# The first batch's prologue by halves of the heads, and the output products of two batches term by term

## The chip, the cores and the metric

The kernel runs on one core of one Trainium2 chip. The metric is the device time of one execution in microseconds (us); lower is better. A core has five engines that run side by side and wait for each other through semaphores: TensorE (PE in the profile; PEld is its loading of weights), VectorE (DVE), ScalarE (ACT), GpSimd (POOL, which does almost nothing here) and SyncE (SP, which here only issues loads and stores). Sixteen DMA engines move data between the chip's main memory and the on-chip memory; loads are issued from SyncE's queue (SPq) or ScalarE's (ACTq). TensorE writes its products into PSUM, which VectorE and ScalarE read.

## The reference

Attention against 32 learned memory slots for each head, followed by a gated feed-forward layer. There are 8 batches, 8 heads, 576 positions and 64 values for each head.

```python
a = phi - np.max(phi, axis=2, keepdims=True)          # (8, 8, 576, 32), over the positions
a = np.exp(a)
a = a / (np.sum(a, axis=2, keepdims=True) + 1e-09)
k_m = np.einsum('bhsm,bhsd->bhmd', a, k)
v_m = np.einsum('bhsm,bhsd->bhmd', a, v)
scores = scale * np.matmul(q, k_m.transpose(0, 1, 3, 2))
scores = scores - np.max(scores, axis=-1, keepdims=True)
attn = np.exp(scores)
attn = attn / (np.sum(attn, axis=-1, keepdims=True) + 1e-09)
attn_out = np.matmul(attn, v_m)
x = attn_out.transpose(0, 2, 1, 3).reshape(B * S, H * D)     # (4608, 512)
h = x @ w_in                                           # (4608, 2048)
g = h * (1.0 / (1.0 + np.exp(-h)))
out = g @ w_out                                        # (4608, 512)
```

w_in (512 x 2048) and w_out (2048 x 512) come as 64-bit floating-point numbers, everything else as 32-bit.

## The kernel before

**Precision.** The large products run in a shortened 32-bit format (fp32r). Each operand is split into a high part and the low rest, and three products stand for one: high by high, high by low, low by high. In the code these are the terms 0, 1 and 2 of `ffn2`: term 0 is g high by w_out high, term 1 g high by w_out low (`wo_lo`), term 2 g low by w_out high. The small products of the attention are plain fp32; in the trace each of them stands as two instructions, a transpose as one.

**Weights.** The two weight matrices are loaded as pairs of 32-bit words in blocks (`w_load`; "i0" is the first block of w_in, "o0" of w_out, each with two parts) and put together on chip by `w_conv`, whose steps are letters: p and c on ScalarE, s (a shift) and a (an addition) on VectorE, and for w_out h (the high part, ScalarE) and l (the low part, VectorE). `I0`, `O0` and `I1` are the first blocks.

**Order of work.** The eight batches are worked through one after the other. For a batch, the attention weights times w_in need only the product of the memory values with w_in (`p_mm`, its splitting `p_split`), and then the hidden product `ffn1` (tile `h`, line 701), the activation (`silu`), its splitting (`split`), and the output products (`main_step`, `ffn2`, line 746) into four PSUM tiles `acc` of 128 positions each. This runs in 16 steps `fc` of 128 hidden values. The output products of one step are issued behind the hidden product of the next (`finish`): in batch 0 in two pairs of tiles, in batch 1 all four tiles together. The other batches use another form of the output product (`st_step`, line 893). The attention of batch b + 1 is worked out in the shadow of batch b.

**The prologue.** For the first batch nothing can hide the attention; it is a prologue, written out by hand. Inside it TensorE, VectorE and ScalarE each keep the order of the program text (`in_order`). The heads are in two groups p (or g) of four: even and odd heads; k, v and q hold the groups side by side: group g of q and of the transposed memory keys lies on partitions 64g to 64g + 63. The steps:

- `load_phi`, `load_kv`, `load_q`: the loads. `load` with `few` waits until the load issued five before it (`DEEP`) has landed. kv is loaded from ScalarE's queue in four chunks of 128 positions (`kv`) and the rest of 64 positions (`kr`), q in two halves of the positions.
- `phi_max`, `phi_allmax`, `phi_sub`, `phi_exp`: the exponential of phi (lines 258 to 323).
- `e_mm` (lines 335 and 345): the sums over the positions of both groups, and their division (lines 353 to 361) into `kvn`.
- `f_tr`, `f_vt`: `kvn` is turned into `kvT` (lines 492 to 500).
- `f_scores(u)` (line 511): the scores of the half u of the positions for all heads.
- `f_copy(u)`, `f_turn(u)` (lines 526 to 545): the scores to SBUF and turned on TensorE, so that positions lie on partitions; the 64 positions beyond 512 (`left`) are handled with u = 1, as a fifth transpose.
- `f_max`, `f_sub`, `f_exp`, `f_sum`, `f_norm` (lines 565 to 586): the soft-max of a half; `f_back` (lines 593 and 601) turns it back; `f_high(u)`, `f_low(u)` (lines 612 to 617) split it into `aparts`, the operand of the first hidden product; u = 2 is the rest.
- `keep_warm(t, n)`: n products of no use, which keep TensorE busy.

Between these steps stand the conversions of the first weights. The allocation of PSUM tiles goes round: the tag `acc` has four buffers, the tags `h` and `bg` one each.

Outside the prologue, TensorE keeps the order of the program in all batches, SyncE and ScalarE in parts; VectorE's order is made by a planner from its own estimates, with `behind` where an order is forced.

## Time and profile before

| | |
|---|---|
| Median of 3 runs | 677.16 us (676.49 to 677.25) |
| Profiled execution, its own time | 677.24 us |
| Its span in the trace | 675.5 us |
| TensorE busy | 665.1 us (98%) |
| VectorE busy | 518.6 us (77%) |
| ScalarE busy | 370.2 us (55%) |
| Granted clock of TensorE | 1.0 |
| Moved by DMA | 93.92 MB |

"Busy" is the time in which an engine has an instruction in hand; TensorE's products overlap and their ends are modelled, so its share says that it is never without work, not that it works at its peak. The trace gives each instruction's start from the beginning of the span, its duration, its line in the kernel, the tiles that it writes and reads, and, where the engine stood idle before it, for how long and what ended that.

### The profile page before, as it was taken

The numbers are of one execution on the slowest core, as the hardware profiler recorded it, in microseconds if no ns is written. First come the engines' busy times: TensorE is split into PE (matmuls) and PEld (weight loads), VectorE is DVE, ScalarE is ACT, GpSimd is POOL, SyncE is SP. The second block draws the span as 40 slices with busy tenths as digits, with TensorE's granted clock in tenths as the row PEclk, the third lists the DMA queues.
The fourth block names the chain that finished last, engine by engine and source line by source line (L and its number), as shares of the span: only waits on it lengthen the run. The fifth ranks groups of instructions, "written<-read, shape, count | busy, mean of one in ns | idle before, by whom it ended". The sixth has DMA issues, their size and how long they took to land.

```text
span 675.5 us, 14539 instructions
## 1 busy us (share of the span) xinstructions
PE 665.1 (98%) x5792; PEld 588.5 (87%) x5792; DVE 518.6 (77%) x1092; ACT 370.2 (55%) x686; POOL 0.7 (0%) x6
## 2 busy tenths in 40 slices
PE   7999999999999999999999999999999999999997
PEld 3587778787869998999988999899997999889996
DVE  3997898889948589868877688877877668867653
ACT  3878684533544556654645546564654646554441
POOL 0000000000000000000000000000000000000000
PEclk9999999999999999999999999999999999999999
DMA  9988985224261552253420534116430304300001
GB/s 335 373 330 293 299 321 184 78 103 157 90 195 47 184 190 93 79 200 119 165 94 17 185 111 172 64 50 230 157 126 33 86 2 157 115 27 17 32 1 48
DMA packets 37907, 93.92 MB, mean 139 GB/s; under 512 B 4688, under 2 KB 21456, under 8 KB 34256
## 3 DMA queue, kind: packets, MB, share of 16 engines
q1 hardware_dynamic: 36816, 90.22, 38.5%
q10 hardware_dynamic: 1024, 2.77, 1.1%
q8 instruction: 46, 0.75, 0.5%
q14 instruction: 21, 0.17, 0.1%
HBM read 77.22 MB, written 15.73 MB: 138 GB/s over the span
## 4 chain that ended last, share of the span: by engine, by line
PE 79%; DVE 6%; issue 1%; ACT 1%; DMA 1%; DVEq 0%; ACTq 0%
PE sum L893 36%; PE h L854 23%; PE lsum L977 5%; PE acc L746 4%; PE bg L649 3%; PE h L701 2%; PE accleft L746 2%; PE bg L382 1%; PE h L335 1%; PE bg L335 1%; PE pacc L649 1%; DMA phi<-in_phi 1%; DVE gparts L720 1%; DVE wf L814 1%; DVE gparts L718 0%
## 5 line engine op out<-in xcount | busy, mean ns | idle before, releaser
L854 PE MATMUL h<-aparts,pm 128*128 128x288 f32 x1152 | 168.5, 295 | 0.0
L854 PEld LDWEIGHTS h<-aparts,pm 128*128 128x128 f32 x1152 | 157.4, 188 | 0.5
L868 ACT ACTIVATE gbuf<-h 128x512 f32<-128x512 f32 x96 | 57.3, 597 | 116.7 <-PE h L854 113.4
L893 PE MATMUL sum<-wo_hi,aparts 128*128 128x256 f32 x384 | 102.3, 289 | 0.0
L893 PE MATMUL sum<-kept,aparts 128*128 128x256 f32 x576 | 100.1, 282 | 0.0
L893 PE MATMUL sum<-wo_lo,aparts 128*128 128x256 f32 x384 | 100.0, 282 | 0.0
L873 DVE TENSOR_TENSOR gbuf<-gbuf 128x256 f32<-128x256 f32 x96 | 40.6, 423 | 68.8 <-ACT gbuf L868 68.4
L882 ACT ACTIVATE aparts<-gbuf 128x512 fp32r<-128x512 f32 x86 | 54.4, 633 | 62.0 <-DVE gbuf L877 62.0
L746 PE MATMUL acc<-wo_hi,gparts 128*128 128x512 f32 x256 | 84.4, 394 | 0.0
L893 PEld LDWEIGHTS sum<-kept,aparts 128*128 128x128 f32 x576 | 82.5, 191 | 0.0
L893 PEld LDWEIGHTS sum<-wo_hi,aparts 128*128 128x128 f32 x384 | 72.7, 189 | 9.8 <-ACT gleft L870 7.5
L884 DVE TENSOR_TENSOR gparts<-gbuf,aparts 128x512 fp32r<-128x512 f32 x86 | 59.6, 693 | 19.8 <-ACT aparts L882 19.8
L893 PE MATMUL sum<-wo_hi,gparts 128*128 128x256 f32 x384 | 73.2, 281 | 0.0
L893 PEld LDWEIGHTS sum<-wo_lo,aparts 128*128 128x128 f32 x384 | 73.1, 190 | 0.0
L893 PE MATMUL sum<-kept,gparts 128*128 128x256 f32 x288 | 65.5, 282 | 0.0
L893 PEld LDWEIGHTS sum<-wo_hi,gparts 128*128 128x128 f32 x384 | 59.4, 190 | 0.0
L746 PEld LDWEIGHTS acc<-wo_hi,gparts 128*128 128x128 f32 x256 | 47.8, 188 | 11.5 <-issue 1.0
L701 PEld LDWEIGHTS h<-aparts,pm 128*128 128x128 f32 x372 | 51.7, 188 | 7.0 <-issue 2.9
L701 PE MATMUL h<-aparts,pm 128*128 128x288 f32 x372 | 56.1, 299 | 0.6 <-DVE aparts L612 0.5
L872 ACT ACTIVATE aparts<-gbuf 128x384 fp32r<-128x384 f32 x96 | 50.4, 525 | 0.0
L746 PE MATMUL acc<-wo_lo,gparts 128*128 128x512 f32 x128 | 49.3, 393 | 0.4 <-DVE wo_lo L182 0.4
L893 PEld LDWEIGHTS sum<-kept,gparts 128*128 128x128 f32 x288 | 47.9, 190 | 0.0
(226 smaller groups left out, 956.6 us busy)
## 6 DMA issues: line engine op xcount, KB each, us to landing
win<-win_saved SPq DMA_DIRECT2D x24, 1024.0 KB, 5.0
kv<-in_kv SPq DMA_DIRECT2D x28, 516.0 KB, 5.0
q<-in_q SPq DMA_DIRECT2D x16, 576.0 KB, 6.2
raw<-in_w_in SPq DMA_DIRECT2D x14, 512.0 KB, 7.4
raw<-in_w_out SPq DMA_DIRECT2D x6, 1024.0 KB, 7.0
win_saved<-win SPq DMA_DIRECT2D x4, 1024.0 KB, 8.6
phi<-in_phi SPq DMA_DIRECT2D x7, 576.0 KB, 8.4
out<-oo SPq DMA_DIRECT2D x26, 128.0 KB, 2.1
```

The costliest lines, as they stand in the source:

```text
L335: nc.tensor.matmul(pt[p][M * r : M * (r + 1), :KVW], e[:, p, c, M * r : M * (r + 1)], kvt[c][:, p, r], start=c == 0, stop=False, skip_grou ...
L649: nc.tensor.matmul((bg[p][M * r : M * (r + 1)] if beside else bg[M * r : M * (r + 1), p, :w]).rearrange("p (k f) -> p k f", f=P), kvT[D * ...
L701: nc.tensor.matmul(h[:, hf, :HALF], wt[:, p, fs], a[:, p, hf * HALF : (hf + 1) * HALF], start=n[hf] == 0, stop=n[hf] == 5, skip_group_chec ...
L746: nc.tensor.matmul(acc[key], gt[:, cs], wt[:, fc], start=fc == 0 and n == 0, stop=fc == NFC - 1 and n == 2)
L854: nc.tensor.matmul(h[:, i, :HALF], wt[:, p, f : f + P], a[:, p], start=n == 0, stop=n == 5)
L868: nc.scalar.activation(gbuf[:, :MAIN].rearrange("p (i f) -> p i f", i=2), h[:, :, :w], AF.Silu)
L872: nc.scalar.activation(hi[:, :3], g[:, 1:4], AF.Copy)
L873: nc.vector.tensor_tensor(g[:, 4:6], g[:, :1].broadcast_to([P, 2, P]), g[:, 1:3], op=ALU.subtract)
L882: nc.scalar.activation(hi[:, 3:], g[:, 4:], AF.Copy)
L884: last_split.append(nc.vector.tensor_tensor(lo[:, 3:], g[:, 4:], hi[:, 3:], op=ALU.subtract))
L893: nc.tensor.matmul(sums[bank][:, place * Q : (place + 1) * Q], gt[:, k], wt, start=bank not in begun, stop=True, skip_group_check=True,)
L977: nc.tensor.matmul(sums[k], part[gt][:, 2 * i + k], wt[:, fc], start=n == 0 and i == 0 and m == 0, stop=True, skip_group_check=True,)
```

## The change

In the prologue the first batch is cut by the two groups of heads instead of by halves of the positions. Group 0's share of kv is loaded first, from ScalarE's queue (`load_kv0(0)`); then, from SyncE's queue and five at a time, group 0's share of q, group 1's share of kv, the first part of i0, group 1's share of q, and the other first weights. A share of a kv chunk has half the bytes in each partition; a share of q and of `kr` lies on 64 partitions.

`e_mm(0)` is replaced by `f_sums(p)` and `f_div(p)`, called for group 0 and later for group 1; all three operations of the division are on VectorE. `f_tr(p)` turns one group with two products by the identity instead of transposes. `f_scores(u)` works on the heads of group u and all positions. The scores' copy goes to `gbuf`. `f_rec` takes the reciprocal of both sums at once, where `f_sum` did it for each half. The text order of the prologue is new, and with it the order on TensorE, VectorE and ScalarE.

`main_step` issues the output products term by term over its tiles in all steps but the last of the first two batches (before: the first three steps of batch 0), and in step 1 and the even steps of batch 0 in the order 0, 2, 1 (before: in steps 1 and 2). In `w_forms`, which prepares another form of w_out in batch 1, one subtraction is put behind another on VectorE.

```diff
--- before.py
+++ after.py
@@ -239,6 +239,26 @@
         t = sb.tile([P, NR, KVW], F32, tag="kr", name=f"kr{b}", bufs=1)
         load(t.rearrange("p r f -> p (r f)"), kv[b, :, FULLC * KVC :], queue=queue)
         at[b]["kr"] = t
+
+    def load_kv0(g, few=False):
+        queue = None if few else nc.scalar
+        if g == 0:
+            at[0]["kv"] = [
+                sb.tile([P, 2, NR, KVW], F32, tag=f"kv{c}", name=f"kv0_{c}", bufs=1) for c in range(FULLC)
+            ]
+            at[0]["kr"] = sb.tile([P, NR, KVW], F32, tag="kr", name="kr0", bufs=1)
+        n = NR * KVW
+        for c in range(FULLC):
+            f = c * KVC + g * n
+            load(at[0]["kv"][c][:, g].rearrange("p r f -> p (r f)"), kv[0, :, f : f + n], few, queue)
+        load(at[0]["kr"][rows(g)].rearrange("p r f -> p (r f)"), kv[0, rows(g), FULLC * KVC :], few, queue)
+
+    def load_q0(g, few=False):
+        for hf in range(2):
+            if g == 0:
+                at[0]["q", hf] = sb.tile([P, NR, HALF], F32, tag=f"q{hf}", name=f"q0_{hf}", bufs=1)
+            d = slice(D * g, D * (g + 1))
+            load(at[0]["q", hf][d].rearrange("p r s -> p (r s)"), qT[0, hf, d], few)
 
     def load_q(b, hf, few=False):
         t = sb.tile([P, NR, HALF], F32, tag=f"q{hf}", name=f"q{b}_{hf}", bufs=1)
@@ -484,34 +504,63 @@
     first = {}
     UW = (2 * HM, 2 * HM + P)
 
-    def f_tr():
+    def f_sums(p):
+        e, er, kvt, kr = (at[0][k] for k in ("e", "er", "kv", "kr"))
+        pt = first["pt", p] = ps.tile([P, 512], F32, tag="acc", name=f"first{p}", bufs=NI)
+        for c in range(FULLC):
+            for r in range(NR):
+                nc.tensor.matmul(
+                    pt[M * r : M * (r + 1), :KVW],
+                    e[:, p, c, M * r : M * (r + 1)],
+                    kvt[c][:, p, r],
+                    start=c == 0, stop=False, skip_group_check=True,
+                )
+        for r in range(NR):
+            nc.tensor.matmul(
+                pt[M * r : M * (r + 1), :KVW],
+                er[rows(p), M * r : M * (r + 1)],
+                kr[rows(p), r],
+                start=False, stop=True, skip_group_check=True,
+            )
+
+    def f_div(p):
+        pt = first["pt", p]
+        rs = sb.tile([P, 1], F32, tag="rs", name="rs", bufs=2)
+        nc.vector.tensor_scalar(rs, pt[:, 2 * D : KVW], EPS, None, op0=ALU.add)
+        nc.vector.reciprocal(rs, rs)
+        src = pt[:, : 2 * D].rearrange("p (k d) -> p k d", k=2)
+        nc.vector.tensor_scalar(kvn[:, :, p], src, rs, None, op0=ALU.mult)
+
+    def f_tr(p):
         pt = ps.tile([P, 512], F32, tag="acc", name="firstt", bufs=NI)
-        t = sb.tile([P, 2, NR, M], F32, tag="kvT", name="kvT0", bufs=2)
-        at[0]["kvT"] = t
+        if p == 0:
+            at[0]["kvT"] = sb.tile([P, 2, NR, M], F32, tag="kvT", name="kvT0", bufs=2)
+        t = at[0]["kvT"]
+        d = slice(D * p, D * (p + 1))
         for kind in range(2):
-            nc.tensor.transpose(
-                pt[:, P * kind : P * (kind + 1)], kvn[:, kind].rearrange("p g d -> p (g d)"), ident
+            nc.tensor.matmul(
+                pt[d, P * kind : P * (kind + 1)], kvn[:, kind, p], ident, start=True, stop=True, skip_group_check=True
             )
-        nc.vector.tensor_copy(t[:, 0].rearrange("p r m -> p (r m)"), pt[:, :P])
-        first["vt"] = t, pt
-
-    def f_vt():
-        t, pt = first["vt"]
-        nc.scalar.copy(t[:, 1].rearrange("p r m -> p (r m)"), pt[:, P : 2 * P])
+        nc.vector.tensor_copy(t[d, 0].rearrange("p r m -> p (r m)"), pt[d, :P])
+        first["vt", p] = t[d, 1], pt[d, P : 2 * P]
+
+    def f_vt(p):
+        t, pt = first["vt", p]
+        nc.scalar.copy(t.rearrange("p r m -> p (r m)"), pt)
 
     def f_scores(u):
         if u == 0:
-            t = [ps.tile([P, 512], F32, tag="acc", name=f"firsts{p}", bufs=NI) for p in range(2)]
+            t = [ps.tile([P, 512], F32, tag="acc", name=f"firsts{hf}", bufs=NI) for hf in range(2)]
         else:
             h = ps.tile([P, 2, 512], F32, tag="h", name="firsts", bufs=1)
-            t = [h[:, p] for p in range(2)]
-        kvT, q = at[0]["kvT"], at[0]["q", u]
+            t = [h[:, hf] for hf in range(2)]
+        d = slice(D * u, D * (u + 1))
         for r in range(NR):
-            for p in range(2):
+            for hf in range(2):
                 nc.tensor.matmul(
-                    t[p][M * r : M * (r + 1), :HALF],
-                    kvT[D * p : D * (p + 1), 0, r],
-                    q[D * p : D * (p + 1), r],
+                    t[hf][M * r : M * (r + 1), :HALF],
+                    at[0]["kvT"][d, 0, r],
+                    at[0]["q", hf][d, r],
                     start=True, stop=True, skip_group_check=True,
                 )
         first["st", u] = t if u == 0 else h
@@ -519,8 +568,8 @@
     def f_copy(u):
         if u == 0:
             first["left"] = sb.tile([P, P], F32, tag="mx", name="sleft", bufs=1)
-        t = first["main", u] = sb.tile([P, 2, 2 * P], F32, tag=f"kv{u}", name=f"sT{u}", bufs=1)
-        left = first["left"].rearrange("p (g h f) -> p g h f", g=2, h=2)[:, :, u]
+        t = first["main", u] = gbuf.rearrange("p (g h f) -> p g h f", g=2, h=2)[:, u]
+        left = first["left"].rearrange("p (g h f) -> p g h f", g=2, h=2)[:, u]
         st = first["st", u]
         if u:
             nc.scalar.copy(t, st[:, :, : 2 * P])
@@ -576,8 +625,10 @@
         nc.scalar.activation(f_sc(u), f_sc(u), AF.Exp, scale=SCALE)
 
     def f_sum(u):
-        sm = f_part(u, "sm", 2 * S // M)
-        nc.vector.tensor_reduce(sm, f_groups(f_sc(u)), op=ALU.add, axis=AX.X)
+        nc.vector.tensor_reduce(f_part(u, "sm", 2 * S // M), f_groups(f_sc(u)), op=ALU.add, axis=AX.X)
+
+    def f_rec():
+        sm = first["sm"]
         nc.vector.tensor_scalar(sm, sm, EPS, None, op0=ALU.add)
         nc.vector.reciprocal(sm, sm)
 
@@ -603,7 +654,7 @@
 
     def f_to(x, u):
         v = at[0][x].rearrange("p g (h f) -> p g h f", h=2)
-        return v[:, :, u, : 2 * P] if u < 2 else v[:, :, :, 2 * P :]
+        return v[:, u, :, : 2 * P] if u < 2 else v[:, :, :, 2 * P :]
 
     def f_high(u):
         if "ahi" not in at[0]:
@@ -764,8 +815,8 @@
             at_ += n
 
     def main_step(b, fc, gs, tiles, terms=None):
-        if b == 0 and fc < 3:
-            for n in terms or ((0, 2, 1) if fc else (0, 1, 2)):
+        if fc < NFC - 1:
+            for n in terms or ((0, 2, 1) if b == 0 and fc and (fc < 3 or fc % 2 == 0) else (0, 1, 2)):
                 for i in tiles:
                     ffn2(gs, slice(i * P, (i + 1) * P), fc, (b, i), (n,))
             return
@@ -818,7 +869,7 @@
             nc.vector.tensor_tensor(b11, b12, b11, op=ALU.subtract)
             nc.vector.tensor_tensor(b12, b22, b12, op=ALU.add)
             nc.vector.tensor_tensor(b22, b22, b11, op=ALU.add)
-            nc.vector.tensor_tensor(b21, b22, b21, op=ALU.subtract)
+            at[0]["last", j] = nc.vector.tensor_tensor(b21, b22, b21, op=ALU.subtract)
             return
         f = at[0]["forms", j].rearrange("p k (q f) -> p (k q) f", q=2)
         t1 = sb.tile([P, 1, DMODEL], F32R, tag="cva1", name="t1", bufs=1)
@@ -833,7 +884,9 @@
         for t, i, e in runs:
             src, to = f[:, n : n + e - i], t[:, i:e]
             nc.scalar.activation(to[:, :, :Q], src, AF.Copy)
-            nc.vector.tensor_tensor(to[:, :, Q:], src, to[:, :, :Q], op=ALU.subtract)
+            lo = nc.vector.tensor_tensor(to[:, :, Q:], src, to[:, :, :Q], op=ALU.subtract)
+            if t is t1:
+                behind(lo.ins, at[0]["last", j])
             n += e - i
         load(saved[j], as_f32(t1[:, 0]))
 
@@ -1152,14 +1205,16 @@
     with in_order(DVE, ACT) as last:
         load_phi(0)
         nc.scalar.activation(tiny[:, :1], ident[:, :1], AF.Exp)
-        load_kv(0)
-        for c in LOADS.split():
-            if c[0] == "Q":
-                load_q(0, int(c[1]), True)
-            elif c[0] == "L":
-                load_next(True)
-            else:
-                w_load((c[0], 0), int(c[1]), True)
+        load_kv0(0)
+        load_q0(0, True)
+        load_kv0(1, True)
+        w_load(I0, 0, True)
+        load_q0(1, True)
+        w_load(I0, 1, True)
+        w_load(O0, 0, True)
+        w_load(O0, 1, True)
+        for _ in range(3):
+            load_next(True)
         keep_warm(idle, 10)
         phi_max(0, (0,))
         phi_allmax(0, (0,))
@@ -1171,44 +1226,48 @@
         for p in range(2):
             phi_exp(0, (p,))
         keep_warm(idle, 2)
-        e_mm(0)
+        f_sums(0)
+        f_div(0)
+        keep_warm(idle, 3)
+        f_tr(0)
+        f_vt(0)
+        keep_warm(idle, 1)
+        f_scores(0)
+        f_copy(0)
+        keep_warm(idle, 1)
+        f_sums(1)
+        f_div(1)
+        f_turn(0)
+        f_tr(1)
+        f_vt(1)
+        f_max(0)
+        f_sub(0)
         w_conv(I0, 0, "pc")
-        keep_warm(idle, 3)
-        f_tr()
-        f_vt()
-        w_conv(I0, 0, "s")
-        keep_warm(idle, 2)
-        f_scores(0)
+        keep_warm(idle, 4)
         f_scores(1)
-        f_copy(0)
-        w_conv(I0, 0, "a")
-        f_turn(0)
+        f_exp(0)
+        w_conv(I0, 0, "sa")
         f_copy(1)
-        f_max(0)
         f_turn(1)
-        f_sub(0)
         spare = ps.tile([P, 512], F32, tag="acc", name="spare", bufs=NI)
-        keep_warm(spare, 3)
-        f_exp(0)
+        keep_warm(spare, 6)
         w_conv(I0, 1, "pc")
+        f_sum(0)
         f_max(1)
         f_sub(1)
         f_exp(1)
         nc.scalar.activation(tiny[:, :1], ident[:, :1], AF.Silu)
-        keep_warm(spare, 13)
-        f_sum(0)
+        w_conv(I0, 1, "sa")
+        bg = p_mm(0, 0, CW, False)
+        keep_warm(spare, 3)
+        f_sum(1)
+        f_rec()
         f_norm(0)
-        w_conv(I0, 1, "sa")
         f_back(0)
-        f_sum(1)
         w_conv(O0, 0, "p")
+        p_split(0, 0, CW, bg, (0,))
+        w_conv(O0, 0, "c")
         f_high(0)
-        w_conv(O0, 0, "c")
-        keep_warm(spare, 3)
-        bg = p_mm(0, 0, CW, False)
-        keep_warm(spare, 5)
-        p_split(0, 0, CW, bg, (0,))
-        w_conv(I1, None, "p")
         f_norm(1)
         f_back(1)
         f_low(0)
@@ -1217,6 +1276,7 @@
         p_split(0, 0, CW, bg, (1,))
         f_high(1)
         w_conv(O0, 0, "h")
+        w_conv(I1, None, "p")
         f_low(1)
         f_low(2)
         w_conv(O0, 0, "a")
```

## The prediction

> **What bounds the kernel now.** I read the page first: the span, and the forty slices of TensorE. Every slice but the first and the last shows nine tenths or more, and the first is the prologue. So TensorE is the bound from the end of the prologue to the end, and whatever the prologue gains or loses goes to the end one to one, unless TensorE finds a new wait or loses an old one.
>
> ```profile
> span 675.5 us, 14539 instructions
> PE   7999999999999999999999999999999999999997
> ```
>
> Then I read the timeline of the first 61 us on TensorE. The columns are start, duration, engine, line, operation, destination and sources, shapes, count, and in brackets the idle time before it with what ended it. In the prologue two loads hold TensorE up (0.46 us for kv, 0.68 us for q); at 26.43 the first hidden product starts, held by a DVE operation; the only wait afterwards in batch 0 is 0.43 us at 60.92, for a low part of w_out.
>
> ```profile
> 9.32 0.87 PE L335 MATMUL first<-kv,phi 128*32 128x129 f32 x24
> 10.65 1.31 PE L335 MATMUL first<-kv,phi 128*32 128x129 f32 x40 [0.46 <-DMA kv<-in_kv]
> 11.89 0.45 PE L345 MATMUL first<-kr,phi 64*32 64x129 f32 x16
> ...
> 14.24 0.72 PE L511 MATMUL firsts<-q,kvT 64*32 64x288 f32 x16
> 15.64 0.72 PE L511 MATMUL firsts<-q,kvT 64*32 64x288 f32 x16 [0.68 <-DMA q<-in_q]
> ...
> 17.21 0.66 PE L543 MATMUL firstu<-ident,sT 128*128 128x128 f32 x4 [0.26 <-ACT sleft L527]
> 17.70 0.27 PE L545 MATMUL firstu<-ident,sleft 128*128 128x128 f32 x1
> ...
> 26.43 2.10 PE L701 MATMUL h<-aparts,pm 128*128 128x288 f32 x12 [0.47 <-DVE aparts L612]
> ...
> 60.92 0.50 PE L746 MATMUL acc<-wo_lo,gparts 128*128 128x512 f32 x1 [0.43 <-DVE wo_lo L182]
> ```
>
> Last I read VectorE and ScalarE between 12 and 29 us, where the start of that product is decided. On VectorE the reader should see that from 16.99 to 26.28 one operation follows the other with no bracket, hence no idle time: the first batch's soft-max is VectorE-bound there.
>
> ```profile
> 12.43 0.22 DVE L353 TENSOR_SCALAR rs<-first 128x1 f32<-128x1 f32 x2 [2.42 <-PE first L345]
> ...
> 12.88 0.35 DVE L361 TENSOR_SCALAR kvn<-first,rs 128x128 f32<-128x128 f32 x1
> 13.90 0.29 DVE L495 COPY kvT<-firstt 128x128 f32<-128x128 f32 x1 [0.67 <-PE firstt L492]
> ...
> 15.44 0.68 DVE L178 CUSTOM_DVE_ANT_0 win<-raw,win 128x1024 uint16<-128x1024 uint16 x1
> 16.99 0.69 DVE L565 TENSOR_REDUCE fmx<-firstu 128x16 f32<-128x512 f32 x1 [0.87 <-PE firstu L543]
> 17.71 0.69 DVE L570 TENSOR_TENSOR fsc<-firstu,fmx 128x512 f32<-128x512 f32 x1
> 18.32 0.81 DVE L565 TENSOR_REDUCE fmx<-firstu 128x20 f32<-128x640 f32 x1
> 19.17 0.82 DVE L570 TENSOR_TENSOR fsc<-firstu,fmx 128x640 f32<-128x640 f32 x1
> ...
> 24.99 0.68 DVE L617 TENSOR_TENSOR aparts<-firsta,aparts 128x512 fp32r<-128x512 f32 x1
> 25.59 0.42 DVE L176 TENSOR_SCALAR cva<-cva 128x512 uint32<-128x512 uint32 x1
> 25.99 0.29 DVE L612 CAST aparts<-firstar 128x128 fp32r<-128x128 f32 x1
> ```
>
> ```profile
> 16.46 0.59 ACT L526 COPY sT<-firsts 128x512 f32<-128x512 f32 x1 [0.72 <-PE firsts L511]
> 16.94 0.22 ACT L527 COPY sleft<-firsts 128x64 f32<-128x64 f32 x1
> 18.44 0.63 ACT L576 ACTIVATE fsc<-fsc 128x512 f32<-128x512 f32 x1 [1.28 <-DVE fsc L570]
> 18.97 0.66 ACT L172 ACTIVATE win<-raw 128x512 f32<-128x512 f32 x1
> ...
> 20.10 0.72 ACT L576 ACTIVATE fsc<-fsc 128x640 f32<-128x640 f32 x1
> 20.84 1.28 ACT L1197 ACT_TABLE_LOAD   x1
> 22.14 0.20 ACT L1197 ACTIVATE tiny<-ident 128x1 f32<-128x1 f32 x1
> 22.25 0.66 ACT L172 ACTIVATE cva<-raw 128x512 f32<-128x512 f32 x1
> 22.82 0.58 ACT L614 ACTIVATE aparts<-firsta 128x512 fp32r<-128x512 f32 x1
> 23.29 0.67 ACT L174 ACTIVATE raw<-raw 128x512 int32<-128x512 uint32 x1
> ```
>
> **The change, part by part: the prologue.** I walk the new order forward from a point that it leaves alone, with the durations and gaps of these rows. The exponentials of the first half end as before, so f_sums(0) starts at 9.32.
>
> *First half up to the scores.* 40 products took 1.24 us (10.65 to 11.89), 0.031 each; 32 make 0.99, and of the 0.45 for 16 products of the rest I take 0.30 for 8: end 10.61. f_div(0): 0.09 to start (11.89 plus 0.45 to 12.43), 0.45 to the multiplication (12.43 to 12.88), 0.35 for it: 11.50. f_tr(0) is now two ordinary fp32 products instead of two transposes. No row shows them; below stands 0.41 (a transpose of 0.27 and half another), above 0.72 (sixteen narrower fp32 products), and I take 0.65, being nearer the fp32 row, and 0.05 to start: 12.20. The copy adds 0.04 and 0.29: 12.53; the scores 0.05 and 0.72: 13.30. They ended at 14.96, so here the change leads by 1.66 us. The kv wait of 0.46 and the q wait of 0.68 are gone.
>
> *Second half before the first maximum.* VectorE's order now puts f_div(1) and the copy of f_tr(1) ahead of f_max(0). f_sums(1) starts about 0.2 after the scores (one warming product): 13.50, ends 14.79; division 0.89: 15.68; f_tr(1) 0.70: 16.38; the copy starts at 16.42, and f_max(0) about 0.25 behind: 16.67. It was 16.99, so the lead has shrunk to 0.32. That is what the halves cost: a second chain of sums, division and turn between the first scores and the first maximum.
>
> *The second half loses its place.* f_sub(0) starts 0.72 after f_max(0), 17.39, and ends 18.08; f_exp(0) 18.12. On ScalarE f_copy(1) is queued behind f_exp(0); before, it ran ahead of it, at 16.46. Start to start after an exponential is 0.53 (18.44 to 18.97): 18.65; the left part 0.48 later, 19.13, ends 19.35. f_turn(1) 0.05 later, 19.40; its fifth transpose 0.49 later, 19.89, ends 20.16. f_max(1) then starts at 20.21, where it stood at 18.32: 1.89 late. f_sub(1) follows in 0.85: 21.06, ends 21.88.
>
> *From there to the hidden product.* f_exp(1) 21.92; the table load 0.74 later, 22.66; the tiny activation 1.30 later, 23.96; O0's first conversion 0.11 later, 24.07; the high part of p_split 0.57 later, 24.64; O0's second conversion 0.47 later, 25.11; f_high(0), which the new order queues behind it, 0.57 later, 25.68, and it ends at 26.26. f_low(0) 26.30; O0's shift 0.60 later, 26.90; f_high(2) 0.40 later, 27.30, ends 27.59; the hidden product 0.15 later (26.28 to 26.43): 27.74. Against 26.43 that is **1.31 us later**. The other branch into it (sum, reciprocal, two multiplications, nine transposes) has from 22.64 to 27.30, 4.7 us, for three passes of 0.69 to 0.82 and two sets of transposes of 0.66 and 0.76: it is covered, with about a microsecond to spare.
>
> *What I cost at nothing.* I0's shift and addition (0.42 as at 25.59, and 0.68 at 15.44) move behind f_sub(0), into VectorE's wait from 18.08 to 20.21; with f_sum(0), about 0.69, they need 1.8 of its 2.1 us. If f_max(1) could start earlier, they would be paid in full. One pair of small operations fewer (f_rec) lies on the covered branch. The sync queue now issues eleven loads up to I0's second part instead of four, at 0.43 us each:
>
> ```profile
> 0.74 0.87 SPq L88 DMA_DIRECT2D phi<-in_phi  x2
> 10.00:20.00 10.00, 8.27 (x123) 4.21 (x116) 5.37 (x15) 5.20 (x14) 0.00 (x0) 1.00 1.05 386
> ```
>
> Seven more issues are 3.0 us of that queue, which is queued behind landings anyway. The second row is that of the windows (the last numbers are granted clock, share of the DMA engines, and GB/s): the DMA engines are full at 386 GB/s, so bytes decide. Through the second half of q the new order moves 4.67 MB (phi 0.59, kv 2.38, I0's first part 0.52, q 1.18), the same as before up to the q wait that ended at 15.64. So that half of q lands at about 15.6, and kv's second half, 1.11 MB ahead of it, at 12.7. They are asked for at about 17.2 (f_scores(1), four warming products behind 16.38) and 13.5: hidden, by 1.6 and 0.8 us. Their failing is a rival below.
>
> **The products by terms.** 27 blocks of 12 products change order (12 in batch 0, 15 in batch 1). A block by terms already stands in batch 0, from 40.27 to 43.05; a block tile by tile comes from the chain that ended last (start, duration, what):
>
> ```profile
> 40.27 1.10 PE L746 MATMUL acc<-wo_hi,gparts 128*128 128x512 f32 x4
> 43.05 1.75 PE L701 MATMUL h<-aparts,pm 128*128 128x288 f32 x12
> 162.80 1.59 PE h L701 x12
> 164.38 2.75 PE acc L746 x12
> ```
>
> 2.78 against 2.75 us: within 0.03, nothing; the bounds are 27 times that, plus or minus 0.8, of which I take none. What it does do is ask later for wo_lo in even steps: fifth of twelve products instead of second, 0.7 us later. The wait at 60.92 was 0.43, so it goes: minus 0.43. Nothing else in batch 0 is late behind it.
>
> **The sum.** The profiled execution took 677.24 us for its span of 675.5 (1.74 around it), and the median of the runs is 677.16, 0.08 less. 677.24 + 1.31 - 0.43 = 678.12, so I say **678.1**. The unknown prices move it: f_tr twice, minus 0.5 to plus 0.15; sums at the slower pace of 24 in 0.87 us, plus 0.3; a conversion more or less in ScalarE's queue, 0.5. This case alone gives 677.3 to 679.1.
>
> **The rivals.** *The lead is kept.* If the second half fits into VectorE's queue without a wait, the stretch of 9.29 us (16.99 to 26.28) grows by I0's 1.10 and loses 0.45 of small operations: 9.94 from 16.67 gives 26.61, the hidden product at 26.76, 677.1. For it: VectorE was the bound there. Against: f_copy(1) behind f_exp(0). If the early links are quicker as well, down to 675.5.
>
> *Faster by the order of the products.* 288 columns cost 1.59/12 and 512 columns 2.75/12, so 0.0083 us of a product don't grow with its width. If that is the return to the same accumulator, and the new order removes it, 324 products save 2.7 us: 675.4. It decides from 0.004 us a product. Against it: the block at 40.27 is no faster.
>
> *The loads of 64 partitions are slow.* q and the rest of kv now come in transfers of 64 partitions, which no row shows. At full rate: the sum above. At half rate the second half of q is delayed by the time of 1.44 MB once more, 3.7 us: it lands at 19.3, the scores end 20.0, f_copy(1) starts at 20.1 instead of 18.65, and 679.6 follows. It decides from 1.6 us of delay. The Trainium skill, SBUF — State Buffer, section on the DMA port swizzle, says that partitions 0 to 63 reach only half of the ports and gives 196 against 328 GB/s; by that estimate q would land 2.5 us later, at 18.1, and the time would be 678.3. No run here shows it yet.
>
> *The clock drops.* TensorE would idle from about 18 to 19.4 and again before 27.7. If that cost the clock, which the windows show at 1.00, the 24 hidden products (1.59 for 12) would take twice as long: 3.2 us more, 681.3. Before, stretches of about half a microsecond did no harm.
>
> **How the numbers follow.** My forecast 0.46; the lead is kept 0.22; slow loads 0.18; order of products 0.07; clock 0.07. 0.2% is 1.35 us, about what this measurement can tell from no change: faster is below 675.8, slower above 678.5. Faster: 0.07 of the order and 0.06 of the kept lead, 0.13. Slower: 0.16 of my forecast's upper part, 0.17 of slow loads, 0.07 of the clock, 0.40. Within: 0.47. Eight times in ten: 676.2 to 680.3, which leaves out the order, the clock and the lowest of the kept lead.
>
> **What would show it.** Right: the first score products end near 13.3, f_max(0) near 16.7, f_max(1) near 20.2 with a bracket naming TensorE, the hidden product near 27.7, no wait for wo_lo near 62. Wrong in the walk: f_max(1) before 19, or f_high(0) held by something other than ScalarE's queue. Wrong in the loads: brackets naming q or kv at L511 or L335. Wrong in the terms: blocks of 12 output products away from 2.75.

## The result, and the profile after

The changed kernel takes 685.11 us (median of 5 runs, 684.05 to 687.04), the kernel before 677.09 us beside it. The ratio is 1.0128, with a 95% interval of 1.0116 to 1.0139: slower by 8.0 us, where 678.1 was forecast and 680.3 was the upper end of the range.

The profiled execution of the changed kernel took 687.04 us, the longest of the five and 1.9 us above the median, with a span of 685.2. So its trace shows the causes somewhat enlarged. Its span, then the timeline of TensorE in the columns of the prediction:

```profile
span 685.2 us, 14529 instructions
```

```profile
8.95 1.09 PE L512 MATMUL first<-kv,phi 128*32 128x129 f32 x32
...
15.42 0.43 PE L512 MATMUL first<-kv,phi 128*32 128x129 f32 x8 [0.40 <-DMA kv<-in_kv]
18.12 0.61 PE L519 MATMUL first<-kr,phi 64*32 64x129 f32 x8 [2.27 <-DMA kr<-in_kv]
...
24.14 1.35 PE L560 MATMUL firsts<-q,kvT 64*32 64x288 f32 x14 [0.55 <-DMA q<-in_q]
...
35.35 2.10 PE L752 MATMUL h<-aparts,pm 128*128 128x288 f32 x12 [1.13 <-DVE aparts L663]
...
70.34 1.21 PE L797 MATMUL acc<-wo_hi,gparts 128*128 128x512 f32 x4 [1.20 <-ACT wo_hi L180]
71.99 0.73 PE L797 MATMUL acc<-wo_lo,gparts 128*128 128x512 f32 x2 [0.44 <-DVE wo_lo L182]
```

Two places hold the difference. The first hidden product starts at 35.35 where it stood at 26.43, 8.92 us later. And near 70 us TensorE waits 1.20 us for the high part of w_out and 0.44 for the low, where it had waited 0.43 in all: 1.21 more. Some shorter waits towards the end of batch 1 are gone (0.39). That makes 9.7 us, and the two spans, 675.5 and 685.2, are 9.7 apart.

The reader should first see the brackets of the prologue: kv, `kr` and q, all loads. `kr`, the last 64 positions, reaches the second group 2.27 us late, and the second q share is there only at 24.14. VectorE shows what follows from it, the two maxima at 21.18 and 27.68 (before: 16.99 and 18.32):

```profile
21.18 0.69 DVE L614 TENSOR_REDUCE fmx<-firstu 128x16 f32<-128x512 f32 x1
...
27.68 0.82 DVE L614 TENSOR_REDUCE fmx<-firstu 128x20 f32<-128x640 f32 x1 [3.32 <-PE firstu L594]
```

Why the loads are late is seen in the windows of 2 us (the last three numbers are the granted clock of TensorE, the busy share of the DMA engines, which is added up from single packets and can come out a little above 1, and GB/s). First before, then after:

```profile
12.00:14.00 2.00, 1.67 (x23) 0.64 (x21) 0.87 (x6) 1.00 (x3) 0.00 (x0) 1.00 1.01 408
...
16.00:18.00 2.00, 1.74 (x26) 1.11 (x11) 1.09 (x3) 0.70 (x2) 0.00 (x0) 1.00 1.07 415
```

```profile
8.00:10.00 2.00, 1.90 (x36) 1.23 (x36) 1.03 (x3) 1.15 (x3) 0.00 (x0) 1.00 0.99 198
...
16.00:18.00 2.00, 0.00 (x0) 0.00 (x0) 0.00 (x0) 0.00 (x0) 0.00 (x0) 1.00 1.12 241
18.00:20.00 2.00, 1.88 (x14) 1.20 (x15) 0.67 (x3) 0.00 (x0) 0.00 (x0) 0.55 1.03 164
```

From 8 to 22 us the DMA engines are busy for 0.83 to 1.12 of the time, nearly as before, and move 164 to 265 GB/s, where they had moved 343 to 415. From 16 to 18 us no computing engine does anything at all.

### The profile page after: what moved, and what is told of

Same layout as the page of the kernel before. It is cut to its first block, busy times and chain, and to the rows that moved or that the text cites. A ratio compares the mean times of both kernels' runs of the same rounds, so it can differ in the third digit from the quotient of the medians.

```text
span 685.2 us, 14529 instructions
## 1 busy us (share of the span) xinstructions
PE 670.0 (98%) x5787; PEld 590.8 (86%) x5787; DVE 519.4 (76%) x1092; ACT 370.3 (54%) x686; POOL 0.7 (0%) x6
## 4 chain that ended last, share of the span: by engine, by line
PE 90%; DVE 2%; ACT 1%; issue 1%; DVEq 0%; ACTq 0%
PE sum L946 36%; PE h L907 22%; PE acc L797 11%; PE h L752 6%; PE lsum L1030 5%; PE bg L700 4%; PE accleft L797 2%; PE bg L355 1%; PE bg L402 1%; PE h L355 1%; PE pacc L700 1%; DVE wf L865 0%; ACT raw L174 0%; DVE kept L887 0%; ACT kept L886 0%
## 5 line engine op out<-in xcount | busy, mean ns | idle before, releaser
L797 PE MATMUL acc<-wo_hi,gparts 128*128 128x512 f32 x256 | 72.3, 396 | 1.2 <-ACT wo_hi L180 1.2
L797 PEld LDWEIGHTS acc<-wo_hi,gparts 128*128 128x128 f32 x256 | 46.0, 188 | 11.7 <-issue 1.9
L936 DVE TENSOR_TENSOR gparts<-gbuf,aparts 128x384 fp32r<-128x384 f32 x86 | 47.4, 551 | 0.1
```

The source lines that it names most:

```text
L797: nc.tensor.matmul(acc[key], gt[:, cs], wt[:, fc], start=fc == 0 and n == 0, stop=fc == NFC - 1 and n == 2)
L936: behind(nc.vector.tensor_tensor(lo[:, :3], g[:, 1:4], hi[:, :3], op=ALU.subtract).ins, s4)
```

## The experiments

All times beside a kernel before of 676.57 to 676.74 us on the same chip; the ratio is to that one.

**1. Full-height loads.** The changed kernel with q in two loads of 128 partitions, and `kr` in one, asked for with the first group; all else as changed. With this the second group's q also moves ahead of its kv in the order.

```diff
 def load_kv0(g):
-    load(kr[rows(g)], kv[0, rows(g), FULLC * KVC :])
+    if g == 0: load(kr, kv[0, :, FULLC * KVC :])
 ...
-load_q0(0); load_kv0(1); w_load(I0, 0); load_q0(1)
+load_q(0, 0); load_q(0, 1); load_kv0(1); w_load(I0, 0)
```

> The changed kernel, but q is loaded in two transfers of 128 partitions (by halves of the positions, at the place of the first group's share) and the rest of kv in one of 128 partitions; kv's four chunks still come by group, in rows of half the length. Theory (height): transfers of 64 partitions move at about half the rate of those of 128; then kv's second share lands near 13 and q by 10.5, TensorE has no wait for a load, keeps its clock, and the first hidden product starts near 27.7 as in my walk: 677.5 to 679.5 us. Rival (depth): half-sized loads at five in flight leave the DMA engines starved; then the loads stay late and the time stays above 683. Rival (rows): kv's shorter rows are slow; then kv's second share still lands after 15 and the time stays above 681.

Measured: 679.76 us, 1.0046 [1.0031, 1.0061], 0.3 us above the theory's upper end and below both rivals' times. Of the 8.0 us, 5 are gone, and with them every load in TensorE's brackets:

```profile
12.51 1.30 PE L561 MATMUL firsts<-q,kvT 64*32 64x288 f32 x16
...
18.44 1.20 PE L561 MATMUL firsts<-q,kvT 64*32 64x288 f32 x16
21.30 1.02 PE L593 MATMUL firstu<-ident,gbuf 128*128 128x128 f32 x4 [1.67 <-ACT sleft L577]
...
30.25 2.10 PE L753 MATMUL h<-aparts,pm 128*128 128x288 f32 x12 [1.13 <-DVE aparts L664]
```

```profile
17.77 0.69 DVE L615 TENSOR_REDUCE fmx<-firstu 128x16 f32<-128x512 f32 x1
...
22.58 0.82 DVE L615 TENSOR_REDUCE fmx<-firstu 128x20 f32<-128x640 f32 x1 [1.25 <-PE firstu L595]
```

```profile
18.76 0.69 ACT L172 ACTIVATE win<-raw 128x512 f32<-128x512 f32 x1 [0.72 <-DMA raw<-in_w_in]
...
19.87 0.65 ACT L626 ACTIVATE fsc<-fsc 128x512 f32<-128x512 f32 x1
20.55 0.59 ACT L576 COPY gbuf<-firsts 128x512 f32<-128x512 f32 x1
```

This is the walk of the prediction with no load that TensorE waits for; ScalarE still waits 0.72 us for I0's. Its hidden product stands at 30.25, not 27.74, and TensorE doesn't keep its clock, as the theory had it: it is at half from 21.4 to 24.9 us. What is still 2.5 us too late can be read step by step; it is done below.

**2. The terms alone.** The kernel before with only the new order of the output products (and the one forced order in `w_forms`).

```diff
-if b == 0 and fc < 3:
-    for n in terms or ((0, 2, 1) if fc else (0, 1, 2)):
+if fc < NFC - 1:
+    for n in terms or ((0, 2, 1) if b == 0 and fc and (fc < 3 or fc % 2 == 0) else (0, 1, 2)):
```

> The kernel before, with only the output products of the first two batches term by term (and the one forced order in the other form of w_out). My reckoning: blocks of 12 products stay at 2.75 us, the wait of 0.43 us for a low part of w_out goes, so 676.7, ratio 0.9994. Rival (accumulators): each block is shorter by up to 0.1 us, 27 of them: 674.5. Rival (planner): the other engines' order changes with it and new waits of about 1 us appear, as the 1.20 us for a high part of w_out that the changed kernel shows near 70: 678.

Measured: 675.85 us, 0.9989 [0.9980, 0.9998], which is 0.76 us less. The wait for `wo_lo` at 60.92 is gone. It is the quickest version of this study, 0.1% below the kernel before.

**3. Half-height q alone.** The kernel before with each q load cut into two of 64 partitions, same bytes, same queue.

```diff
-load(t, qT[b, hf], few)
+for g in range(2):
+    load(t[D * g : D * (g + 1)], qT[b, hf, D * g : D * (g + 1)], few)
```

> The kernel before, with each of the two q loads of the first batch cut into two transfers of 64 partitions, nothing else. Theory (height): the 1.18 MB of q take twice their time, some 3 us more, so the second scores start near 18.5 instead of 15.64 and the time is 679 to 680.5. Rivals (depth, rows): q's rows are as long as before and the bytes in flight hardly fewer, so no more than 0.5 us: 677.1 to 677.6.

Measured: 682.74 us, 1.0087 [1.0072, 1.0102]: cutting four transfers out of two costs 6 us, more than the 2.4 to 3.9 us of my theory. The windows, then TensorE:

```profile
12.00:14.00 2.00, 1.63 (x8) 0.50 (x6) 1.18 (x5) 1.68 (x4) 0.00 (x0) 1.00 1.05 233
14.00:16.00 2.00, 1.00 (x16) 0.21 (x14) 0.27 (x1) 0.34 (x3) 0.00 (x0) 1.00 1.02 233
```

```profile
14.91 0.71 PE L516 MATMUL firsts<-q,kvT 64*32 64x288 f32 x14 [0.62 <-DMA q<-in_q]
16.17 0.64 PE L516 MATMUL firsts<-q,kvT 64*32 64x288 f32 x2 [0.54 <-DMA q<-in_q]
17.39 0.71 PE L516 MATMUL firsts<-q,kvT 64*32 64x288 f32 x14 [0.58 <-DMA q<-in_q]
...
28.73 2.10 PE L706 MATMUL h<-aparts,pm 128*128 128x288 f32 x12 [0.47 <-DVE aparts L617]
```

While q is under way the rate is 233 GB/s with all engines busy; before, the same two windows had 408 and 374. The trace's single packets say the same: one of 4608 bytes, one partition of q, takes 180 ns (median) at full height and 331 at half height. That puts the hidden product 2.3 us later. Near 60 us the same two waits as in the changed kernel have come in (1.2 for `wo_hi`, 1.1 for `wo_lo`), another 1.9. This profiled execution is 1.4 us below the median of its four; what the others have more, no trace shows.

**4. Eight loads under way.** The changed kernel with `DEEP` 8 for 5: is it only that too few loads are under way?

```diff
-DEEP = 5
+DEEP = 8
```

> The changed kernel with eight loads in flight instead of five. Theory (height): the rate is set by the height of the transfers, not by their number, so 683 to 686. Rival (depth): the engines are fed, kv's and q's second shares land by 13 and 16, and the time falls to 678 to 680.

Measured: 684.89 us, 1.0126 [1.0102, 1.0150]: the time doesn't change. With more loads sharing the engines, the late `kr` is merely that of the first group:

```profile
13.38 0.66 PE L519 MATMUL first<-kr,phi 64*32 64x129 f32 x8 [1.77 <-DMA kr<-in_kv]
```

The equal time is a sum, though: in this trace the first hidden product starts 1.8 us earlier than in the changed kernel's (33.57) and the waits near 70 us are not there, but the first twelve hidden products run at half clock (3.22 us for 2.10).

**5. Filled gaps.** The changed kernel with more products of no use in the gaps of the prologue, against the drop of the clock (0.55 from 18 to 20 us above).

```diff
-keep_warm(idle, 4)
+keep_warm(idle, 12)
 f_scores(1)
+keep_warm(spare, 5)
 ...
-keep_warm(spare, 6)
+keep_warm(spare, 12)
```

(and nine inside `f_sums(1)`, ahead of its products with `kr`)

> The changed kernel with more products of no use in TensorE's gaps: 9 ahead of the rest of the second group's sums, 12 instead of 4 ahead of the second scores, 5 behind them, 12 instead of 6 behind their turn. Theory (clock): the granted clock, 0.50 to 0.59 in parts of 18 to 32 us, stays near 1.00, the turn, the scores and the first product with w_in take 0.66, 1.20 and 0.66 instead of 1.11, 1.35 and 1.11, and the time falls by 1 to 2.5 us, to 682.6 to 684. Rival (loads alone): those steps have slack behind the loads of kv and q, and the time stays within 0.7 of 685.

Measured: 685.96 us, 1.0130 [1.0114, 1.0145]: no better, and above what either the theory or the rival had said. The clock is at 1.00 in all windows from 8 to 34 us, but the fills themselves now hold the path: `kr` landed at 15.3 and its products start behind the fills at 18.63, the last of q landed at 20.9 and the second scores start behind the fills at 23.38, both without a wait. And the half clock is put off, not avoided. It comes from 34.4 to 37.8 us, where the products set the time:

```profile
34.01 2.91 PE L754 MATMUL h<-aparts,pm 128*128 128x288 f32 x12 [1.13 <-DVE aparts L665]
```

So this run doesn't tell what the drop costs the prologue; behind it the late drop takes 0.8 us of the first twelve hidden products alone (2.91 for 2.10).

**6. The copy ahead of the exponential.** Experiment 1 with `f_copy(1)` ahead of `f_exp(0)`, and the first part of I0's conversion behind both. The prediction held f_copy(1)'s place behind f_exp(0) for the reason of its 1.31 us.

```diff
-w_conv(I0, 0, "pc")
 keep_warm(idle, 4)
 f_scores(1)
-f_exp(0)
-w_conv(I0, 0, "sa")
 f_copy(1)
+f_exp(0)
+w_conv(I0, 0, "pcsa")
```

> The kernel of e1_full_height with ScalarE's order changed: the copy of the second scores ahead of the first exponential, the first conversion of i0 behind it. Theory (place in the queue, from my walk): the turn of the second scores starts 0.8 to 1.5 us earlier than the 21.30 of e1, f_max(1) with it, and the time is 678.3 to 679. Rival (VectorE's order): f_max(1) still stands behind I0's shift and addition and f_sum(0), which now wait for later inputs, and nothing is gained or it is lost: 679.5 to 680.5.

Measured: 682.31 us, 1.0082 [1.0068, 1.0096], so 2.5 us slower than experiment 1. The transposes come 0.8 us earlier (20.53), as the theory had it, but the maximum behind them comes later, 23.50 for 22.58. VectorE:

```profile
21.72 0.43 DVE L176 TENSOR_SCALAR win<-win 128x512 uint32<-128x512 uint32 x1 [2.51 <-ACT win L172]
...
23.50 0.82 DVE L615 TENSOR_REDUCE fmx<-firstu 128x20 f32<-128x640 f32 x1
```

In VectorE's fixed order I0's shift stands ahead of `f_max(1)`, and it now waits 2.51 us for the conversion that was moved back on ScalarE. The rival had the mechanism: one queue was relieved and the next one held the same step. But it had allowed 680.5 at most, and that step is 0.9 of the 2.5 us. The rest goes with the clock. While VectorE is late, TensorE stands idle for 3.79 us, and from 28.0 to 34.8 us it is at half clock: from f_max(1) to the hidden product 8.18 us pass in place of 7.67, and the first twelve hidden products take 3.22 in place of 2.10. A version with I0's shift and addition behind `f_max(1)` as well was not tried.

**7. q ahead of I0.** Experiment 2 with both q loads asked for ahead of I0's first part, to take away the q wait of the kernel before.

```diff
-LOADS = "i0 Q0 Q1 i1 o0 o1 L L L"
+LOADS = "Q0 Q1 i0 i1 o0 o1 L L L"
```

> The kernel of e2_terms_only with q's two loads ahead of the first part of i0. If the loads set the prologue's pace, kv's rest lands about 0.7 us earlier and q 1.3 us earlier, the wait of 0.68 us for q goes, and the first hidden product starts 0.5 to 1 us earlier: 674.9 to 675.4, faster than the kernel before by 0.2%. If VectorE's stretch from f_max(0) on sets it, I0's shift and addition come later into that stretch and take the gain back: 675.5 to 676.3.

Measured: 676.92 us, 1.0003 [0.9994, 1.0012]: 1.1 us slower than experiment 2, which neither theory said. The q wait is gone, but q now takes the engines from kv on the other queue, which is needed first:

```profile
11.10 1.31 PE L335 MATMUL first<-kv,phi 128*32 128x129 f32 x40 [1.06 <-DMA kv<-in_kv]
...
13.22 0.46 PE L345 MATMUL first<-kr,phi 64*32 64x129 f32 x16 [0.82 <-DMA kr<-in_kv]
```

**8. The exponential behind the high part.** The waits near 70 us come from an order on ScalarE, called the flip below. Before, `wo_hi` was rounded ahead of the table load and the next batch's exponential; after, it stands behind both. First before, then after:

```profile
58.22 1.06 ACT L180 ACTIVATE wo_hi<-cva 128x1024 fp32r<-128x1024 f32 x1 [0.24 <-DVE cva L176]
59.30 1.28 ACT L319 ACT_TABLE_LOAD   x1
```

```profile
64.83 1.28 ACT L339 ACT_TABLE_LOAD   x1
66.12 1.17 ACT L339 ACTIVATE phi<-phi 128x1152 f32<-128x1152 f32 x1
...
69.24 1.04 ACT L180 ACTIVATE wo_hi<-cva 128x1024 fp32r<-128x1024 f32 x1
```

No line of the change touches this order. The changed kernel with the old order forced:

```diff
 i = nc.scalar.activation(at[b]["et"], at[b]["et"], AF.Exp)
+if b == 1:
+    behind(i.ins, last_high[0])
```

> The changed kernel with one order forced on ScalarE: the second batch's exponential of phi behind the rounding of the high part of w_out that stands near it, as in the kernel before. Theory (planner): the waits of 1.20 and 0.44 us near 70 go, 683.2 to 684. Rival (DMA): the conversion was waiting for its load, the waits stay, 685.

Measured: 683.90 us, 1.0099 [1.0083, 1.0115]. Both waits are gone, and the median is 1.2 us lower. The same flip is in experiments 3, 5 and 9, and not in 1, 2, 4, 6, 7 and 10 to 12; what tips it was not found.

The prologue of this run is that of the changed kernel, and its trace is a second look at it:

```profile
15.65 0.42 PE L522 MATMUL first<-kr,phi 64*32 64x129 f32 x8
...
20.84 3.44 PE L563 MATMUL firsts<-q,kvT 64*32 64x288 f32 x16 [2.23 <-DVE win L177]
...
34.16 2.10 PE L755 MATMUL h<-aparts,pm 128*128 128x288 f32 x12 [1.13 <-DVE aparts L666]
```

Here `kr` is in time. The second q share is late again: its two loads landed at 20.70 and 22.07 (the bracket names I0's shift, which ended just after the first of them landed). So the 2.27 us of waiting for `kr` belong to one execution; q is late in both.

**9. Only q at full height.** Experiment 1 with `kr` again in two loads of 64 partitions, one with each group.

```diff
-if g == 0: load(kr, kv[0, :, FULLC * KVC :])
+load(kr[rows(g)], kv[0, rows(g), FULLC * KVC :])
```

> The changed kernel with q alone loaded whole (two transfers of 128 partitions, in place of group 0's share); the remainder kr stays in two loads of 64 partitions, one per group. The version with q and kr both whole took 679.8 us, the changed kernel 685.1. Theory (it is 64-partition rows times bytes that cost: q is 1.15 MB of them, kr 0.26 MB): 680.2 to 681.2, with the second group's sums kept from kr by less than 0.6 us (2.27 in the changed kernel). Rival (kr's second half, last in its queue, is what holds the path): the wait for kr stays over 1.2 us and the time is 682 or more. If kr is of no account at all: 679.8 within 0.4.

Measured: 682.68 us, 1.0091 [1.0073, 1.0109]. The rival's two conditions are met, a time over 682 and a wait for `kr` over 1.2 us, against my theory, which counted bytes of half height. Both signs are weak: the time holds the flip, some 1.2 us, and this profiled execution is the longest of its six, 686.19.

```profile
18.27 0.42 PE L519 MATMUL first<-kr,phi 64*32 64x129 f32 x8 [1.94 <-DMA kr<-in_kv]
```

**10. `kr` in halves, but early.** Is it the height of `kr` or its place, last of its group? Experiment 9 with both halves asked for one behind the other, with the first group.

```diff
-load(kr[rows(g)], kv[0, rows(g), FULLC * KVC :])
+for s in range(2) if g == 0 else ():
+    load(kr[rows(s)], kv[0, rows(s), FULLC * KVC :])
```

> The kernel with q whole and kr in halves (682.7 us) with the second half of kr asked for right behind the first, on ScalarE's queue and not last of the second group's loads on the sync queue. Both halves are still transfers of 64 partitions, counted as one load. With kr in one transfer of 128 partitions at that place the time was 679.8. Theory (kr costs by its place: fifth of its group, its issue waits for the landing of a share of q): the second sums' wait for kr of 1.94 us goes, and the time is 679.8 within 0.8. Rival (kr costs by its height of 64 partitions): a wait for kr or kv over 1 us stays in the first or second sums, and the time is 681.5 or more.

Measured: 680.31 us, 1.0053 [1.0041, 1.0066], within the interval of experiment 1. The wait is gone though the halves are still of 64 partitions. So where `kr` is late, its place does it and not its height. Last of five, it may be issued only when group 0's share of q has landed, because of the rule of five under way. SyncE's queue of the changed kernel shows it, `kr` issued at 12.59, while kv began at 7.69:

```profile
5.13 1.96 SPq L88 DMA_DIRECT2D q<-in_q  x2
7.69 3.92 SPq L88 DMA_DIRECT2D kv<-in_kv  x4
12.59 0.47 SPq L88 DMA_DIRECT2D kr<-in_kv  x1
```

Of the 2.4 us between experiments 9 and 10, some 1.2 are the flip, which only the former has. How much of the rest is `kr` stays open, as in experiment 8 it was in time at the late place.

**11 and 12. Shorter rows.** The loads changed in another way too: kv comes in eight loads of half the row length. The kernel before with that alone, and then with each pair counted as one load in the rule of five.

```diff
-load(t, kv[b, :, c * KVC : (c + 1) * KVC])
+for g in range(2):
+    load(t[:, g], kv[b, :, c * KVC + g * KVC // 2 : c * KVC + (g + 1) * KVC // 2])
+    if g == 0: loads.pop()          # only in the second of the two
```

> The kernel before with each of the first batch's four big kv loads cut into two by groups of heads: still 128 partitions, same queue and order, but eight loads with rows of half the length in place of four. It is the other thing that the change does to the loads. Theory (only the height of a transfer matters): 676.6 within 0.4, the kv share of the window from 8 to 12 us still over 370 GB/s. Rival (shorter rows or more transfers are slow by themselves): slower by 1 us or more, with the sums waiting for kv by over 0.8 us more in sum than before.

> The kernel before with the first batch's four big kv loads cut into two by groups of heads, as in the run that took 678.8 us, but each pair counted as one in the rule that a load waits for the landing of the fifth load before it. There, I0's first part was issued at 8.62 (before: 5.91) and q from 9.62 (before: 7.97). Theory (the rule counts transfers, so smaller transfers leave fewer bytes under way and hold q back; short rows themselves cost nothing): the issues go back to about 6 and 8, the wait for q goes from 2.3 us to under 1.2, and the time to 676.7 within 0.6. Rival (short rows or more transfers are slow by themselves): the time stays at 678.2 or more.

Measured: 678.78 us, 1.0023 [1.0013, 1.0033], and 677.39 us, 1.0010 [1.0000, 1.0019]. The first is 2.0 us slower than before, against my 0.4; and yet kv itself is not late, TensorE runs through its 64 products without a wait. It is q that is late (2.3 us of waiting), as it was issued later. SyncE's queue of the one and of the other:

```profile
8.62 0.38 SPq L88 DMA_DIRECT2D raw<-in_w_in  x1
9.62 1.01 SPq L88 DMA_DIRECT2D q<-in_q  x2
```

```profile
5.95 0.38 SPq L88 DMA_DIRECT2D raw<-in_w_in  x1
7.38 1.62 SPq L88 DMA_DIRECT2D q<-in_q  x2
```

A rule that counts loads lets half the bytes be under way when the loads are half as large. With the pairs counted as one, the q wait is gone and 1.2 of the 2.0 us with it. These 1.2 us go with the clock: of the nine executions of experiment 11, the four with a mean granted clock of 0.997 to 1.000 took 677.0 to 677.6 us, the five at 0.995 or 0.996 took 678.8 to 679.4, and in its trace TensorE is at half clock from 15.8 to 22.7, from within the wait for q on. In experiment 12, nine of eleven were at 0.999 or 1.000, with 676.7 to 677.9 (the other two, at 0.997, took 678.1 and 678.8). At full clock the two versions differ no more than their own executions do. What remains over the kernel before, 0.8 us (interval 0.0 to 1.3), is at the edge of what I had allowed; there TensorE waits 1.65 us for `kr`, which still stands last in its queue, behind eight loads.

## Why the prediction was wrong

**The step that failed: "hidden, by 1.6 and 0.8 us".** The loads were costed at nothing because "the DMA engines are full at 386 GB/s, so bytes decide". They are nearly as busy after the change, at 164 to 265 GB/s. Q's second half was to land at 15.6 and was there at 24.14, in the trace of experiment 8 at 22.07. Kv's second half was to land at 12.7, and its last part, `kr`, let TensorE go on at 18.12 (in experiment 8 at 15.65, in time). Experiment 3 shows the mechanism by itself, 1 and 9 what undoing it is worth: experiment 1 is 4.9 us quicker than the changed kernel, with the flip gone too. Of these, q's height, with the earlier place of its second share, is 2.1 to 2.4 us (685.11 to 682.68, the flip being in both), and the place and height of `kr` together 2.9, of which 1.2 is the flip.

The rival named it ("the loads of 64 partitions are slow") and put its half rate about right, but sized it at 679.6. It delayed one landing once, by 1.44 MB. In the run the first slow loads also hold back what is queued behind them: `kr` waits for group 0's share of q to land, the second share of q is issued behind `kr` at 13.73, and each of these starts late by the delays ahead of it. With a landing at 19.3 in that rival, and 24.1 in the trace, it was 4.8 us short (2.8 by the trace of experiment 8). The Trainium skill, SBUF — State Buffer, section on the DMA port swizzle, gives 196 against 328 GB/s for 64 against 128 partitions, a ratio of 0.60; the trace agrees, with 233 (experiment 3) against 374 to 408 GB/s (before) and 331 against 180 ns for a packet. The 678.3 that I drew from it had the same fault as the rival: one delay, where there is a chain of them.

**The walk itself: half right.** Experiment 1 is its test (its first sums start at 9.18, mine at 9.32):

| step | predicted | experiment 1 |
|---|---|---|
| f_tr(0), duration | 0.65 | 0.65 |
| f_scores(0), start | 12.58 | 12.51 |
| f_scores(0), duration | 0.72 | 1.30 |
| f_sums(1), start | 13.50 | 14.06 |
| f_max(0) | 16.67 | 17.77 |
| f_exp(0) | 18.12 | 19.87 |
| f_copy(1) | 18.65 | 20.55 |
| f_max(1) | 20.21 | 22.58 |
| h, first hidden product | 27.74 | 30.25 |
| from f_max(1) to h | 7.53 | 7.67 |

- Mis-sized terms: the scores and the sums behind them. I took 0.72 from sixteen instructions (eight products) of the same shape before; they take 1.20 to 1.30 when all of them use the same 64 partitions. Before, the two groups took turns. The second sums take 1.77 us (14.06 to 15.83), where I had 1.29. Each makes f_max(0) about 0.5 us late, together 1.1.
- Missing term: f_exp(0) stands behind I0's conversion on ScalarE, which waited for its load until 18.76 (bracket 0.72). The exponential then started not 1.45 us behind f_max(0), as in the walk, but 2.10; I had this only among the unknown prices, with 0.5.
- f_copy(1) behind f_exp(0) is as predicted: 0.68 later, predicted 0.53.
- The clock: the transposes of f_turn(1) ran at half of it and the fifth of them took its start 0.82 us behind the first, not 0.49.
- From the second maximum on, the walk is right within 0.14 us at the hidden product and 0.21 on the way. The 0.2 us come from the branch that I had called covered, "with about a microsecond to spare": the transposes that f_high(0) reads end at 28.20, and it starts at 28.24, 0.76 behind O0's second conversion and not 0.57.

That experiment 6 could not win by moving the copy shows that the place of f_copy(1), which I gave as the reason, is one of two queues that hold the same step. VectorE's order is the other: I had cost I0's shift and addition at nothing there, and had noted that they would be paid in full if f_max(1) could start earlier.

**The products by terms: right, with a mis-sized gain.** Blocks keep their pace. From the chain that ended last, after:

```profile
44.36 2.74 PE acc L797 x12
```

The gain is 0.76 us (0.14 to 1.35 by the interval) against 0.43; shorter waits towards the end of batch 1 may be some of the rest (0.39 us in the traces after and of experiment 2). In the changed kernel it is hidden, since the flip of ScalarE's order puts 1.64 us of waiting at the same place. "Nothing else in batch 0 is late behind it" was wrong there: an order made elsewhere had moved.

**The sum of the medians.** The walk without TensorE's waits for loads and without the terms costs 3.9 us (3.15 for experiment 1 and 0.76 back), terms -0.76, q's height 2.1 to 2.4, `kr` 1.7, the flip 1.2: 8.1 to 8.4, against 8.0 measured. The split between `kr` and the flip is the least sure, as the runs of one of these kernels scatter by as much (681.3 to 686.2 in experiment 9). The parts are differences of neighbouring versions, so that they add up is no test of them, and none is free of the clock. The traces part the time in another way, at the first hidden product:

| trace | first hidden product | from there to the end |
|---|---|---|
| before | 26.43 | 649.0 |
| experiments 1, 2, 7, 8 | 30.25, 25.84, 27.52, 34.16 | 647.9 |
| experiments 4, 6, 10 (first hidden products at half clock) | 33.57, 31.68, 29.83 | 648.8 to 649.0 |
| after (flip) | 35.35 | 649.8 |
| experiment 9 (flip, and half clock) | 33.82 | 650.5 |

Behind the prologue the flip is 1.9 us in these traces and the half clock about 1.0. Of the 9.7 us between the spans before and after, 8.9 lie ahead of the first hidden product and 0.8 behind it, the flip less what the terms save.

**The rivals.** The lead was not kept. The order of the products changes no pace. The clock did drop, behind TensorE's waits, for loads after and for ScalarE in experiment 1. In the trace after it dropped in the prologue and not on the hidden products (2.10 for twelve, as before). In experiments 4, 6, 9 and 10 it did on the first twelve of them, for 1.1 us and not the 3.2 of the rival, so other executions of the changed kernel may pay that too.

## What to carry to other kernels

Where a load is cut, look at its height before its bytes: here 64 partitions moved at 0.57 to 0.62 of the rate of 128, with DMA engines that look just as busy, and what was queued behind them was late as well. A limit on loads under way that counts transfers shrinks when they are cut, and the last small piece of a group (`kr`) can be the one that the consumer waits for; ask for it early. A wait of TensorE can cost more than its length, through the clock (experiments 6 and 11). And when a step is late in one in-order queue, look for its place in the others before moving it: moving the copy on ScalarE only showed VectorE's order.

## What the runs showed of the hardware

- Eight fp32 products on 64 partitions (sixteen instructions) take 0.72 us when they alternate between the two halves of the partitions and 1.20 to 1.30 when all use the same half, at full clock and with no load to wait for. The Trainium skill, TensorE: Matmul & The Clock Gate, section on packing small matmuls, describes products on different row groups of the array that run at the same time; the two rows here agree.
- The granted clock falls to 0.50 for 3.41 us at a time, or two or three times that (21.4 to 24.9 us in experiment 1, 28.0 to 34.8 in 6, 20.6 to 30.9 in 8), and also after gaps that are shorter than this. In experiment 1, in the 3.41 us ahead of the fall, TensorE had been busy for half the time (the window's sum below), and its longest gap was 1.67.

```profile
18.05:21.46 3.41, 1.69 (x19) 1.00 1.01 386
```

  The Trainium skill, TensorE: Matmul & The Clock Gate, part on the HAM clock gate, speaks of an idle window of about 3.4 us; the length agrees, but a window that was half idle was enough here.
- Two loads from different queues share the engines, so that a load moved ahead in one queue delays another queue's (experiment 7: kv and `kr` 1.88 us of waiting, before 0.46).
